# Attention: VectorE's conversions and low parts stand one at a time behind the masks of three steps of a pair, not three in a row in its first step

## The chip, the cores and the metric

The kernel runs on one core of a Trainium2 chip. The metric is the device time of one execution in microseconds (us); for the kernel before it is 1143.96, the median of three runs (1143.52 to 1143.96). Engines are named as in the profile: PE is TensorE (its weight loads are PEld), DVE VectorE, ACT ScalarE, POOL GpSimd, SP SyncE, which here only issues transfers.

## What is computed

Attention with a threshold (scores more than tau below the row's maximum are dropped), then two feed-forward layers on the result.

```python
# q, k, v: (4, 8, 576, 64)
scores = scale * np.matmul(q, k.transpose(0, 1, 3, 2))
thresh = np.max(scores, axis=-1, keepdims=True) - tau
scores = np.where(scores >= thresh, scores, -1000000000.0)
attn = np.exp(scores - np.max(scores, axis=-1, keepdims=True))
attn = attn / (np.sum(attn, axis=-1, keepdims=True) + 1e-09)
x = np.matmul(attn, v)               # then (2304, 512), heads side by side
# first layer:  x = (sigmoid(x @ w_gate) * (x @ w_val)) @ w_out,  d_ff 1536
# second layer: h = x @ w_in;  g = h, 0 or (h + 1)^2 / 4 by range;  out = g @ w_out,  d_ff 2048
```

The weights come as 64-bit floats and are read as pairs of 32-bit words. The kernel makes 32-bit floats of them itself, and splits operands of the feed-forward layers into a high part and a low part (value minus high part).

## The kernel before

**Pairs and steps.** Two heads make a pair; there are 16 pairs, 0 to 15. The 576 rows of a head are four blocks of 128 and a rest of 64, so a pair has five steps, u = 0 to 4; in the last one the rests of both heads share a block. The loop of `attention` (L388 on) runs over steps t = 5p + u, 80 in all and some to drain. It is a pipeline over three steps. In step t stand, on their engines:

- TensorE: the scores of step t (L252; L248 in step 4), the *turns* of step t - 2 (transposes of the probabilities p, L295, and of their last 64 columns lt, L296), and part of the product with v of an earlier block (`attend`, L319).
- VectorE: the *maxima* of step t (L261, one instruction a head: it scales the scores out of PSUM into s and takes the row maximum), then the *masks* of step t - 1 (L281, one a head: threshold, times the exponent, row sum). In step 1 a reciprocal (L333) stands between them.
- ScalarE: the copies of the transposed blocks (L301, L305; L310, L311), the exponents of step t (L273), the copies out of the product with v (L329).
- GpSimd: a shift of the maxima by tau (L264), the copy of the mask's last columns into lt (L288), and the normalisation (L350) two pairs later.

Scores use two banks (wa, wb) in every step, so those of step t + 1 overwrite a bank once VectorE's maxima of step t have read it. Step 4 has one maxima instruction, and step 0 one mask instruction, for the predecessor's step 4; its turns stand in step 1.

**Work beside it.** Weights of the first layer are converted during the attention, six pieces of 128 x 512, by the generator `background` (L352): ScalarE takes out the high words (`extract`, L145, in step 2 of every second pair), and `convert` makes six VectorE instructions of a piece: L155, L157, L159, L161, L165, L169, each building on the one before. Two raw tiles alternate (`load_w`, L129). A call of `next(bg)` advances the generator to its next `yield`. In the loop such a call stands in step 0 of pairs 1 to 12, between the maxima and the mask, and advances by three instructions, so a piece takes two pairs: L155, L157, L159 in the odd one, L161, L165, L169 in the even one.

In pairs 13 to 15 the loop hands out a "gap" at the same place, and `ffn` fills it with VectorE's half of splits: low parts of x (L477, 128 x 768) two in pair 13 and two in pair 14, of weights (L192, 128 x 512) three in pair 15. ScalarE's half, the high parts, was issued at the end of the step ahead (step 4 of pairs 12, 13 and 14). The engines run their instructions in the order of the program; nothing reorders them.

Of the kernel before, what the change touches and what calls it, by code (L numbers as in the profile page):

```python
# [29 lines left out]
def kernel(  # L30
# [57 lines left out]
    high0 = const.tile([P, KD * P], F32, name="high0")  # L88
# [7 lines left out]
    w32 = {(0, 0, 0): ring[0], (0, 0, 1): ring[1]}  # L96
# [12 lines left out]
    def run(*gens):  # L109
        for g in gens:  # L110
            for _ in g:
                pass
# [28 lines left out]
    def extract(ph, gs, c):  # L141

        n = KD * P
        for i, g in enumerate(gs):
            nc.scalar.activation(  # L145
                c[:, i * n : (i + 1) * n], raws[ph, g][:, :, 1].bitcast(F32), AF.Copy, scale=2.0**-112
            )

    def convert(ph, gs, c, a):


        n = KD * P
        c, a = c[:, : len(gs) * n], a[:, : len(gs) * n]
        cu, au = c.bitcast(U32), a.bitcast(U32)
        nc.vector.tensor_scalar(c, c, -DBL_TOP, DBL_TOP, op0=ALU.max, op1=ALU.min)  # L155
        yield
        nc.vector.tensor_scalar(au, cu, 3, None, op0=ALU.logical_shift_left)  # L157
        yield
        nc.vector.scalar_tensor_tensor(au, cu, 0x80000000, au, op0=ALU.bitwise_and, op1=ALU.bitwise_or)  # L159
        yield  # L160
        nc.vector.tensor_scalar(cu, au, 0xFF800000, None, op0=ALU.bitwise_and)  # L161
        yield
        for i, g in enumerate(gs):
            ci = c[:, i * n : (i + 1) * n]
            nc.vector.scalar_tensor_tensor(  # L165
                ci, raws.pop((ph, g))[:, :, 0], 2.0**-52, ci, op0=ALU.mult, op1=ALU.mult
            )
            yield
        nc.vector.tensor_tensor(a, a, c, op=ALU.add)  # L169
        yield  # L170
# [29 lines left out]
    def attention():  # L200
# [14 lines left out]
        U = nf + 1  # L215
        N = NP * U
# [135 lines left out]
        def background():  # L352

            for g in range(2):
                load_w(0, g)
            yield
            for g in range(6):
                extract(0, (g,), high0)
                yield
                n = KD * P  # L360
                ops = convert(0, (g,), high0, w32[0, 0, g // 3][:, g % 3 * n : (g % 3 + 1) * n])
                run(itertools.islice(ops, 3))
                yield
                run(ops)
                if g + 2 < 6:
                    load_w(0, g + 2)
                yield

        def warm(n):

# [13 lines left out]
        bg = background()  # L384
# [7 lines left out]
        for t in range(N + 9):  # L392
            p, u = divmod(t, U)
            on = t < N
            mk = divmod(t - 1, U) if 1 <= t <= N else None
            at = divmod(t - 2, U) if 2 <= t <= N + 1 else None

            pd, ud = divmod(t - U, U)
            pd2, ud2 = divmod(t - 2 * U, U)
            if ud2 in (2, 3) and 0 <= pd2 < NP:  # L400
                normalise(pd2, ud2 - 2)
            if on:
                scores(p, u)
            if t == N + 1:
                yield t - N, True
            if at:
                turns(*at)
            if ud == 2 and 0 <= pd < NP:
                nc.tensor.transpose(left[: 2 * nf + 1, P : 2 * P], sums[pd % 2], ident)
            for part in parts.get(t, ()):  # L410
                attend(*part)
            if on:
                maxima(p, u)
            if at:
                copies(*at)
            if on:
                exponents(p, u)
            if ud == 1 and 0 <= pd < NP:
                denom(pd)
            if on and u == 0 and p > 0:  # L420
                if p < 13:
                    next(bg, None)
                else:
                    yield t - N, "gap"
            if ud == 2 and 0 <= pd < NP:
                sum_rows(pd)
            for part in parts.get(t, ()):
                if part[2][-1] == nf:
                    drain(*part[:2])
            if mk:  # L430
                masks(*mk)
                if mk[1] == nf:
                    nc.gpsimd.tensor_scalar(sums[mk[0] % 2], sums[mk[0] % 2], 1e-9, None, op0=ALU.add)
            if on:
                if u == 1 and p + 1 < NP:
                    corner(p + 1)
                if u == 2 and p + 2 < NP:
                    load(p + 2)
                if u == 4 and p + 2 < NP:
                    load_v(p + 2)  # L440
                if t == 1 or u == 2 and p % 2 == 0 and p < 12:
                    next(bg, None)
            if ud == 3 and 0 <= pd < NP:
                spread(pd)
            if t == N - 1:
                wides[:] = [wb, wa, wt]
            if t == N:
                run(bg)
                nc.scalar.activation(dummy, half, AF.Sigmoid)
                st1.close()  # L450
            if t == N + 2:
                st2.close()
                ps_o.close()
            yield t - N, False

    def ffn(att):


        with ExitStack() as st:
# [340 lines left out]
                            up(0, 0, 0, n, i, pv[i], [kk])  # L800
                        yield

            early, taken, xops = {}, [], {}
            more = first_up()
            ahead = [split_xs(0, 0, 0, T, [c]) for c in range(KD)] + split_list(0, 0, 0, False)
            second = iter(())
            for step, free in att:
                if free == "gap":
                    for g in begun:
                        run(g)  # L810
                    continue
                if free:
                    late = sb("late", 1)
                    wins.append(late.tile([P, 4 * KD * P], F32R, name="win_1"))
                    wouts.extend(late.tile([P, 2, DM], F32R, name=f"wout_{i}") for i in (1, 2))
                    hp_ = sb("hp_", 2)
                    pools["words"] = cv("words", 1).tile([P, 12 * KD * P], F32, name="words")
                    pools["n"] = 0
                    for _, _, gs in todo[:2]:
                        for g in gs:  # L820
                            load_w(0, g)
                    continue
                if step in (-16, -11, -6):
                    begun, ahead = (ahead[:2], ahead[2:]) if step < -6 else (ahead, [])
                    for g in begun:
                        next(g)
                if step == 1:
                    second = split_parts(0, 0, 1, False)
                if step >= 0:
                    run(itertools.islice(second, 2))  # L830
                    run(itertools.islice(more, {0: 4, 1: 2, 2: 2}.get(step, 0)))
# [7 lines left out]
            n = 2 * KD * P  # L839
            slots = [wmore[:, i * n : (i + 1) * n] for i in range(4)] + [x[:, :n] for x in ring]  # L840
            n = 3 * KD * P
# [7 lines left out]
            for s in range(NS):  # L849
                nxt = order[s + 1] if s + 1 < NS else None  # L850
                ops = 8 if order[s][1] == 0 else 6
# [25 lines left out]
                _, t, f = order[s - 1]  # L877
# [74 lines left out]
```

## Time and profile before

| | |
|---|---|
| median of three runs | 1143.96 us |
| profiled execution | 1143.82 us |
| its span, first to last instruction | 1142.0 us |
| busy: PE, DVE, ACT, POOL | 1109.9, 849.0, 620.9, 138.1 us |
| attention, pairs 1 to 15 | 20.4 to 283.7 us of the span |

The profile has pages of totals and views of the trace. A row of a timeline gives the start in us from the span's start, the duration, the engine, the line of the kernel, the operation with its tiles and sizes, and the count of instructions merged in the row; in brackets stands the engine's idle time just before it and what ended that. Matmuls are pipelined and their ends are modelled, so starts are to be trusted more than durations on PE.

### The profile page before, as it was taken

The page shows a single profiled execution, that of the slowest core. Times are in us where ns is not written, and L with a number is a line of the kernel's source. Part 1 is how long each engine was busy: PE and PEld are TensorE (multiplying, and loading weights), DVE is VectorE, ACT ScalarE, POOL GpSimd, SP SyncE. Part 2 cuts the span into 40 slices and gives each one's busy share as a digit, 9 for nine tenths or more (in the row PEclk, how much of TensorE's full clock was granted, in tenths as well). Part 3 has the DMA queues.
Part 4 walks back from the last instruction along what each step waited for, and adds up shares of the span by engine and source line. Part 5 has one row for each costly group of instructions (what it writes and reads, how often), then busy time and mean ns, then how long its engine had stood idle before and what let it go on. Part 6 is the DMA issues. An engine that isn't in the chain of part 4 may idle for free.

```text
span 1142.0 us, 17341 instructions
## 1 busy us (share of the span) xinstructions
PE 1109.9 (97%) x6372; PEld 944.5 (83%) x6372; DVE 849.0 (74%) x1484; ACT 620.9 (54%) x1048; POOL 138.1 (12%) x315
## 2 busy tenths in 40 slices
PE   8999999999799999999999999989999999999998
PEld 5555656556699999999999999988888888988887
DVE  6888888888499999767777762576677767676663
ACT  5777777787444344333344322366566655656553
POOL 3444544555100000000000000000000000000000
PEclk9999999999999999999999999999999999999999
DMA  4323233220665566455446524032312432143301
GB/s 131 88 76 89 78 81 78 62 71 21 212 205 177 176 199 231 168 183 178 154 161 212 176 78 162 19 111 86 133 67 104 156 121 97 72 161 114 111 20 55
DMA packets 65141, 139.09 MB, mean 122 GB/s; under 512 B 9616, under 2 KB 35872, under 8 KB 65056
## 3 DMA queue, kind: packets, MB, share of 16 engines
q1 hardware_dynamic: 64912, 137.98, 36.1%
q8 instruction: 50, 0.82, 0.3%
q14 instruction: 35, 0.29, 0.1%
q10 hardware_dynamic: 144, 0.00, 0.0%
HBM read 111.15 MB, written 26.81 MB: 121 GB/s over the span
## 4 chain that ended last, share of the span: by engine, by line
PE 85%; DVE 8%; ACT 3%; issue 2%; DMA 1%; SPq 0%; POOL 0%; DVEq 0%; POOLq 0%; ACTq 0%
PE y L743 15%; PE pu L610 14%; PE y L761 13%; PE pgv L486 8%; PE pgv L485 8%; PE pgv L487 8%; PE av L319 6%; PE w L295 5%; PE w L252 5%; DVE s L261 2%; PE w L248 2%; DVE p L281 1%; DVE high L165 1%; ACT sqs L619 1%; ACT sqs L620 1%
## 5 line engine op out<-in xcount | busy, mean ns | idle before, releaser
L485 PE MATMUL pgv<-xflat,win 128*128 128x384 f32 x560 | 188.5, 337 | 5.9 <-ACT act L541 3.8
L486 PE MATMUL pgv<-xflat,win 128*128 128x384 f32 x560 | 188.4, 336 | 0.1
L743 PE MATMUL y<-wout,hh 128*128 128x512 f32 x576 | 185.4, 397 | 3.0 <-ACT hh L628 3.0
L487 PE MATMUL pgv<-xflat,win 128*128 128x384 f32 x560 | 188.3, 336 | 0.0
L761 PE MATMUL y<-hh,wout 128*128 128x512 f32 (+1 forms) x576 | 146.7, 337 | 0.0
L261 DVE TENSOR_SCALAR_CACHE_REDUCE s<-w,nscale 128x576 f32<-128x576 f32 x144 | 112.7, 816 | 33.6 <-PE w L252 23.8
L743 PEld LDWEIGHTS y<-wout,hh 128*128 128x128 f32 x576 | 108.9, 189 | 28.0 <-ACT hh L628 3.3
L545 DVE TENSOR_TENSOR act<-pgv,act 128x384 f32<-128x384 f32 x70 | 38.9, 556 | 104.2 <-PE pgv L487 103.9
L743 PE MATMUL y<-wout,hl 128*128 128x512 f32 x288 | 114.3, 397 | 0.5 <-DVE hl L629 0.5
L485 PEld LDWEIGHTS pgv<-xflat,win 128*128 128x128 f32 x560 | 105.9, 189 | 7.9 <-ACT act L541 4.1
L281 DVE SCALAR_TENSOR_TENSOR p<-s,mx,ex 128x576 f32<-128x576 f32 x144 | 112.1, 812 | 0.5 <-POOL lt L288 0.5
L541 ACT ACTIVATE act<-pgv 128x384 f32<-128x384 f32 x70 | 34.2, 489 | 137.1 <-PE pgv L487 136.8
L273 ACT ACTIVATE ex<-s,mx 128x576 f32<-128x576 f32 x144 | 104.8, 775 | 7.2 <-DVE s L261 6.8
L486 PEld LDWEIGHTS pgv<-xflat,win 128*128 128x128 f32 x560 | 106.0, 189 | 2.0 <-DVE xflat L477 0.4
L761 PEld LDWEIGHTS y<-hh,wout 128*128 128x128 f32 x576 | 98.1, 188 | 11.3
L610 PE MATMUL pu<-xflat,win 128*128 128x384 f32 x576 | 105.1, 337 | 1.0 <-DVE sqs L689 0.7
L487 PEld LDWEIGHTS pgv<-xflat,win 128*128 128x128 f32 x560 | 106.0, 189 | 0.0
L546 ACT ACTIVATE hh<-act 128x384 fp32r<-128x384 f32 x72 | 38.0, 527 | 121.7 <-DVE act L545 121.3
L610 PEld LDWEIGHTS pu<-xflat,win 128*128 128x128 f32 x576 | 100.6, 188 | 2.4 <-DVE sqs L689 1.4
L295 PEld LDWEIGHTS w<-ident,p 128*128 128x128 f32 x576 | 62.8, 141 | 41.6 <-ACT ex L273 36.6
L761 PE MATMUL y<-hl,wout 128*128 128x512 f32 (+1 forms) x288 | 97.1, 337 | 0.0
L301 ACT ACTIVATE r<-w 128x1024 f32<-128x1024 f32 x64 | 65.7, 1026 | 49.7 <-PE w L295 49.6
(140 smaller groups left out, 1928.6 us busy)
## 6 DMA issues: line engine op xcount, KB each, us to landing
wmore<-saved SPq DMA_DIRECT2D x32, 512.0 KB
words<-in_moe_w_out_dram SPq DMA_DIRECT2D x26, 512.0 KB
tsum<-tsaved SPq DMA_DIRECT2D x24, 512.0 KB
wmore<-saved SPq DMA_DIRECT2D x15, 768.0 KB
words<-in_moe_w_in_dram SPq DMA_DIRECT2D x16, 512.0 KB
saved<-w SPq DMA_DIRECT2D x16, 512.0 KB
w<-saved SPq DMA_DIRECT2D x16, 512.0 KB
w<-saved SPq DMA_DIRECT2D x9, 768.0 KB
```

Source lines behind the costliest of these rows:

```text
L261: nc.vector.tensor_scalar(t[:, e], w[:, :, :HS], nscale, None, op0=ALU.mult, op1=ALU.min, accum_out=mx[:, 0, e : e + 1])
L273: nc.scalar.activation(ex[:, e], t[:, e], AF.Exp, scale=-1.0, bias=mx[:, 0, e : e + 1])
L281: nc.vector.scalar_tensor_tensor(pr[:, e], t[:, e].rearrange("p a b -> p (a b)"), mx[:, 1, e : e + 1], ex[:, e].rearrange("p a b -> p (a b ...
L295: nc.tensor.transpose(wt[:, e, cs], pr[:, e, cs], ident)
L301: nc.scalar.activation(rt[r].rearrange("p e c n -> p (e c) n")[:, :, o : o + P], wt.rearrange("p e (c n) -> p (e c) n", n=P), AF.Copy,)
L319: nc.tensor.matmul(av[e * D : e * D + D, :n], vs[p % 3][:, e, c], rt[r][:, e, c] if c < nf else rl[r], start=c == 0, stop=c == nf,)
L485: nc.tensor.matmul(ps, ih[:, i, kk], xh[:, kk, c], start=(kk == 0), stop=False)
L486: nc.tensor.matmul(ps, ih[:, i, kk], xl[:, kk, c], start=False, stop=False)
L487: nc.tensor.matmul(ps, il[:, i, kk], xh[:, kk, c], start=False, stop=(kk == KD - 1))
L610: nc.tensor.matmul(ps[bank], l[:, k], r[:, k], start=bool(new) and k == m == 0, stop=k == HK - 1 and m == 2, skip_group_check=True,)
L743: nc.tensor.matmul(y[b], l[:, ts_], r, start=first and m == 0, stop=last and m == 2)
L761: nc.tensor.matmul(at(y, a, b), l[:, ds_], r[:, c], start=new and m == 0, stop=last and m == 2, skip_group_check=True,)
```

## The change

The calls leave step 0's place between maxima and mask. They stand behind the masks now, in steps 0, 3 and 4 of a pair, from t = 3 on, and `background` yields after each single instruction of `convert`. The six instructions of a piece begin in step 3 of the pair in which it was extracted; a piece still ends in step 0 of pairs 2, 4, ... 12. The next raw tile's load is issued with the next extraction (step 2) instead of behind the sixth instruction (step 0). For the low parts the "gap" comes from t = 63 on in the same three steps, and one part is taken each time.

```diff
--- before.py
+++ after.py
@@ -358,13 +358,9 @@
                 extract(0, (g,), high0)
                 yield
                 n = KD * P
-                ops = convert(0, (g,), high0, w32[0, 0, g // 3][:, g % 3 * n : (g % 3 + 1) * n])
-                run(itertools.islice(ops, 3))
-                yield
-                run(ops)
+                yield from convert(0, (g,), high0, w32[0, 0, g // 3][:, g % 3 * n : (g % 3 + 1) * n])
                 if g + 2 < 6:
                     load_w(0, g + 2)
-                yield
 
         def warm(n):
 
@@ -417,11 +413,6 @@
                 exponents(p, u)
             if ud == 1 and 0 <= pd < NP:
                 denom(pd)
-            if on and u == 0 and p > 0:
-                if p < 13:
-                    next(bg, None)
-                else:
-                    yield t - N, "gap"
             if ud == 2 and 0 <= pd < NP:
                 sum_rows(pd)
             for part in parts.get(t, ()):
@@ -431,6 +422,11 @@
                 masks(*mk)
                 if mk[1] == nf:
                     nc.gpsimd.tensor_scalar(sums[mk[0] % 2], sums[mk[0] % 2], 1e-9, None, op0=ALU.add)
+            if on and u in (0, 3, 4) and t > 2:
+                if t <= 12 * U:
+                    next(bg, None)
+                else:
+                    yield t - N, "gap"
             if on:
                 if u == 1 and p + 1 < NP:
                     corner(p + 1)
@@ -800,14 +796,14 @@
                             up(0, 0, 0, n, i, pv[i], [kk])
                         yield
 
-            early, taken, xops = {}, [], {}
+            early, taken, xops, begun = {}, [], {}, []
             more = first_up()
             ahead = [split_xs(0, 0, 0, T, [c]) for c in range(KD)] + split_list(0, 0, 0, False)
             second = iter(())
             for step, free in att:
                 if free == "gap":
-                    for g in begun:
-                        run(g)
+                    run(*begun[:1])
+                    del begun[:1]
                     continue
                 if free:
                     late = sb("late", 1)
```

VectorE's instructions in steps 0 and 1 around pair 5, before (s, mx: maxima; p, sum: masks; high, w: conversions):

```order
L261 TENSOR_SCALAR s,mx_77<-w_126,nscale 128x576
L261 TENSOR_SCALAR s,mx_77<-w_127,nscale 128x576
L155 TENSOR_SCALAR high_84<-high_84 128x512
L157 TENSOR_SCALAR w_0_82<-high_84 128x512
L159 SCALAR_TENSOR_TENSOR w_0_82<-high_84,w_0_82 128x512
L281 SCALAR_TENSOR_TENSOR p,sum_80<-s,mx_76,ex 128x576
L261 TENSOR_SCALAR s,mx_76<-w_126,nscale 128x576
```

The same place now, first step 0, then steps 3 and 4 (between them stand the maxima and masks of steps 1 to 3):

```order
L261 TENSOR_SCALAR s,mx_77<-w_126,nscale 128x576
L261 TENSOR_SCALAR s,mx_77<-w_127,nscale 128x576
L281 SCALAR_TENSOR_TENSOR p,sum_80<-s,mx_76,ex 128x576
L159 SCALAR_TENSOR_TENSOR w_0_82<-high_84,w_0_82 128x512
L261 TENSOR_SCALAR s,mx_76<-w_126,nscale 128x576
```

```order
L281 SCALAR_TENSOR_TENSOR p,sum_81<-s,mx_77,ex 128x576 x2
L161 TENSOR_SCALAR high_84<-w_0_82 128x512
L261 TENSOR_SCALAR s,mx_77<-w_126,nscale 128x576
L281 SCALAR_TENSOR_TENSOR p,sum_81<-s,mx_76,ex 128x576 x2
L165 SCALAR_TENSOR_TENSOR high_84<-raw_86,high_84 128x512
L261 TENSOR_SCALAR s,mx_76<-w_126,nscale 128x576
```

L155 and L157 moved ahead, to steps 3 and 4 of pair 4; L159 stands behind the mask; L161 and L165, which stood in pair 6, follow in steps 3 and 4 of pair 5.

VectorE in step 0 of pair 13, before (xflat: low parts of x):

```order
L261 TENSOR_SCALAR s,mx_77<-w_126,nscale 128x576
L261 TENSOR_SCALAR s,mx_77<-w_127,nscale 128x576
L477 TENSOR_TENSOR xflat<-xall,xflat 128x768 x2
L281 SCALAR_TENSOR_TENSOR p,sum_80<-s,mx_76,ex 128x576
L261 TENSOR_SCALAR s,mx_76<-w_126,nscale 128x576
L261 TENSOR_SCALAR s,mx_76<-w_127,nscale 128x576
```

VectorE from step 3 of pair 13 to step 1 of pair 14, now (the low parts have line 473 in the changed file):

```order
L261 TENSOR_SCALAR s,mx_76<-w_126,nscale 128x576
L261 TENSOR_SCALAR s,mx_76<-w_127,nscale 128x576
L281 SCALAR_TENSOR_TENSOR p,sum_81<-s,mx_77,ex 128x576 x2
L473 TENSOR_TENSOR xflat<-xall,xflat 128x768
L261 TENSOR_SCALAR s,mx_77<-w_126,nscale 128x576
L281 SCALAR_TENSOR_TENSOR p,sum_81<-s,mx_76,ex 128x576 x2
L261 TENSOR_SCALAR s,mx_76<-w_126,nscale 128x576
L261 TENSOR_SCALAR s,mx_76<-w_127,nscale 128x576
L281 SCALAR_TENSOR_TENSOR p,sum_81<-s,mx_77,ex 128x576
L473 TENSOR_TENSOR xflat<-xall,xflat 128x768
L261 TENSOR_SCALAR s,mx_77<-w_126,nscale 128x576
```

The second low part of pair 13 moved from step 0 to step 3; the first one of pair 14 stands behind the mask of step 0.

SyncE's transfers between the loads of v and the spreading of the reciprocals (rb), in pairs 1 and 2, before:

```order
L236 DMA v_164<-in_v_dram 64x64
L129 DMA raw_86<-in_moe_w_out_dram 128x1024
L340 DMA dr<-row_79 9x128
L226 DMA qk<-in_q_dram 128x576
L227 DMA qk<-in_k_dram 128x576
L346 DMA rb<-dr 128x1x512
```

And now:

```order
L236 DMA v_164<-in_v_dram 64x64
L340 DMA dr<-row_79 9x128
L226 DMA qk<-in_q_dram 128x576
L227 DMA qk<-in_k_dram 128x576
L129 DMA raw_86<-in_moe_w_out_dram 128x1024
L346 DMA rb<-dr 128x1x512
```

The raw tile's load moved behind the reciprocals' rows (dr) and the loads of q and k; the same holds for four such loads in all.

## Rows read from the trace of the kernel before

**Rows 1.** Stretches: length, busy us (instructions) by engine, granted clock, DMA share, GB/s.

```profile
...
20.40:283.70 263.30, 250.37 (x1770) 155.78 (x1770) 232.63 (x603) 197.34 (x372) 125.48 (x282) 1.00 0.26 70
...
313.50:318.00 4.50, 4.47 (x16) 4.30 (x17) 3.84 (x5) 1.90 (x4) 0.00 (x0) 0.62 1.02 325
...
```

**Rows 2.** Groups of PE in 20.4 to 283.7 us: busy, mean ns | idle before.

```profile
...
L295 PE MATMUL w<-ident,p 128*128 128x128 f32 x540 | 74.2, 278 | 12.9 <-DVE p L281 10.1 <-ACT ex L273 2.8
...
```

**Rows 3.** Timeline of PE, pairs 1, 5, 6 and 13.

```profile
...
25.99 0.63 PE L295 MATMUL w<-ident,p 128*128 128x128 f32 x4 [0.97 <-DVE p L281]
...
90.76 1.24 PE L252 MATMUL w<-qk 64*128 64x288 f32 x8
91.94 1.09 PE L295 MATMUL w<-ident,p 128*128 128x128 f32 x8
92.87 0.27 PE L296 MATMUL left<-ident,lt 128*128 128x128 f32 x1
...
94.08 1.24 PE L252 MATMUL w<-qk 64*128 64x288 f32 x8
96.01 0.63 PE L295 MATMUL w<-ident,p 128*128 128x128 f32 x4 [0.69 <-DVE p L281]
96.47 0.27 PE L296 MATMUL left<-ident,lt 128*128 128x128 f32 x1
...
106.37 1.04 PE L295 MATMUL w<-ident,p 128*128 128x128 f32 x8
...
108.14 1.24 PE L252 MATMUL w<-qk 64*128 64x288 f32 x8
...
113.65 0.63 PE L295 MATMUL w<-ident,p 128*128 128x128 f32 x4 [0.95 <-DVE p L281]
...
236.26 0.63 PE L295 MATMUL w<-ident,p 128*128 128x128 f32 x4 [0.90 <-ACT ex L273]
...
```

**Rows 4.** Timeline of DVE, pairs 1, 5, 6 and 13.

```profile
...
22.02 0.82 DVE L261 TENSOR_SCALAR_CACHE_REDUCE s<-w,nscale 128x576 f32<-128x576 f32 x1
...
93.52 0.42 DVE L155 TENSOR_SCALAR high<-high 128x512 f32<-128x512 f32 x1
...
94.43 0.69 DVE L159 SCALAR_TENSOR_TENSOR w<-high,w 128x512 uint32<-128x512 uint32 x1
95.04 0.81 DVE L281 SCALAR_TENSOR_TENSOR p<-s,mx,ex 128x576 f32<-128x576 f32 x1
...
106.57 0.82 DVE L261 TENSOR_SCALAR_CACHE_REDUCE s<-w,nscale 128x576 f32<-128x576 f32 x1 [0.49 <-PE w L248]
...
107.32 0.82 DVE L281 SCALAR_TENSOR_TENSOR p<-s,mx,ex 128x576 f32<-128x576 f32 x1
...
108.06 0.82 DVE L281 SCALAR_TENSOR_TENSOR p<-s,mx,ex 128x576 f32<-128x576 f32 x1
...
109.41 0.82 DVE L261 TENSOR_SCALAR_CACHE_REDUCE s<-w,nscale 128x576 f32<-128x576 f32 x1 [0.53 <-PE w L252]
...
110.89 0.42 DVE L161 TENSOR_SCALAR high<-w 128x512 uint32<-128x512 uint32 x1
111.35 0.69 DVE L165 SCALAR_TENSOR_TENSOR high<-raw,high 128x512 f32<-128x512 uint32 x1
...
112.68 0.81 DVE L281 SCALAR_TENSOR_TENSOR p<-s,mx,ex 128x576 f32<-128x576 f32 x1
...
233.56 1.82 DVE L477 TENSOR_TENSOR xflat<-xall,xflat 128x768 fp32r<-128x768 f32 x2
...
```

**Rows 5.** Timeline of POOL, pair 5.

```profile
...
106.22 0.29 POOL L288 COPY lt<-p 128x128 f32<-128x128 f32 x1 [0.73 <-DVE p L281]
107.57 0.71 POOL L264 TENSOR_SCALAR mx<-mx,tau_b 128x1 f32<-128x1 f32 x1 [1.06 <-DVE s L261]
...
```

**Rows 6.** Timeline of ACT, pair 5.

```profile
...
94.14 1.44 ACT L273 ACTIVATE ex<-s,mx 128x576 f32<-128x576 f32 x2
...
105.14 1.44 ACT L273 ACTIVATE ex<-s,mx 128x576 f32<-128x576 f32 x2
...
```

## The prediction

> **What bounds the kernel now.** I read the stages first: busy time and granted clock of each engine in the attention's fifteen pairs after the first, 20.4 to 283.7 us [rows 1]. TensorE is busy for 250.37 of 263.30 us there, at full clock, so 12.93 us is all that TensorE can gain in the stage by waiting less; VectorE is at 232.63, close, but not full. The second view, TensorE's groups of the same stretch, says where the 12.93 us lie: 12.9 stand before the turns (L295) and 10.1 of these were ended by a VectorE mask (L281) [rows 2]. The third view is TensorE's timeline of pair 5 [rows 3]. Call the starts of its five steps S0 to S4: the scores open a step. From S0 = 90.76 to S1 = 94.08 TensorE has no gap. In step 1 the scores start at 94.08, the turns could follow at 95.25 (in step 0 they follow 1.18 us after the scores' start: 91.94 - 90.76), but start at 96.01. From there to the next pair at 108.14 no gap is marked. So each pair waits once, in step 1, for the mask of the pair's predecessor.
>
> VectorE's timeline says why [rows 4]: between the two maxima of step 0 and that mask stand three conversions, 93.52 to 95.04, and the mask can start only then. In even pairs the three take 110.89 to 112.68, 1.79 us for 1.52, and the wait is 0.95 for 0.69 [rows 3, 4]. In pairs 13 to 15 low parts stand there (two in 1.82 us at 233.56, wait 0.90) [rows 3, 4].
>
> **The change part by part.** *Removed: the wait in step 1.* The mask now follows the maxima at once. In pair 5 it starts at 93.52 instead of 95.04 and is over, by its own 0.74 us from start to the next start (its neighbour L281 at 107.32 hands over at 108.06), at 94.26. The turns followed the mask's start by 0.97 (112.68 to 113.65), so they could start at 94.49, and TensorE reaches them at 95.25. The whole wait goes, with 0.76 us to spare. Sum over the pairs of the recorded waits: pair 1 0.97, five odd pairs 0.69, six even 0.95, pairs 13 to 15 0.90 to 0.97: 12.9. A recorded wait counts from the modelled end of the scores, 1.24 us after their start, while TensorE goes on after 1.18 when nothing is in the way; that is some 0.06 to 0.07 more a pair, 1.0 in all. **Gain 13.9 us.** TensorE is next in every step of the pair; I looked at each of the moved instructions for one that takes its place.
>
> *Added in step 0, behind the mask:* one conversion of at most 0.69 us (L159), from 94.26 to 94.95. The next maxima wait for their scores until some 95.35 (scores 94.08, and 1.27 to 1.28 from scores to maxima, as 108.14 to 109.41). Hidden, 0.4 us spare.
>
> *Added in step 3, behind two masks:* L155 or L161, 0.42 us, taking 0.46 with its hand-over (110.89 to the next conversion at 111.35). VectorE idles 0.49 us there, before the maxima at 106.57. Hidden. A low part in its place (0.91 each) makes those maxima 0.3 to 0.4 late, in three places.
>
> *Added in step 4:* L157 (0.45 with its hand-over, 0.91 less 0.46) or L165 (0.69, 0.72 with its hand-over) into an idle time of 0.53 before 109.41. L165 starts at 108.80, lasts until some 109.52 and makes the maxima 0.1 late in the odd pairs. A late maximum costs TensorE nothing until it holds up the scores of the step after: the maxima of 109.41 end by 110.89, and the scores that overwrite their banks stand at 111.46 or later (3.32 after 108.14). 0.1 fits, and so does 0.3 in step 3, where one maximum ends at 107.32 and the next scores stand at 108.14. I take zero; the bound, if the late maxima of the low parts show in full, is 1 us.
>
> *Moved in the first pair.* Two conversions now stand in steps 3 and 4 of pair 0. There VectorE is the bound: the maxima at 22.02 follow a mask without a marked idle time [rows 4]. So the two, 0.91 us with their hand-overs (93.52 to 94.43), push the maxima of pair 1's step 0 to 22.9, their end to 24.4 and the scores of step 1 to some 24.4 to 24.6; the turns then start at about 25.6 instead of 25.99 [rows 3]. Of the 1.04 us that I counted for pair 1 only 0.4 is left: **loss 0.65 us**, between 0 and 0.9.
>
> *Moved on SyncE:* four of the weight loads (512 KB) stand two steps later, behind the q and k loads and ahead of the reciprocals' spreading. The tile is read two pairs later, the spread rows four steps later, and the moved load waits for nothing by then (its buffer's last reader ran three steps before). Nothing; what it could cost is a late spread, in at most four pairs.
>
> *GpSimd.* It copies the last columns of a mask (L288, lt) for TensorE and shifts the maxima (L264). A small operation with nothing beside it takes 0.29 us (106.22); one that began at 107.57 inside the mask of 107.32 took 0.71, to 0.22 us after that mask was over [rows 4, 5]. So an operation with two inputs in SBUF on VectorE holds GpSimd up. The Trainium skill says so too ("SBUF — State Buffer", "Who interferes with whom"): a VectorE instruction with two SBUF inputs, or a tensor_scalar in the two-port mode, and a GpSimd instruction exclude each other for the whole instruction. By that rule this change puts a blocker right where the copy of lt starts, which speaks against it. In this kernel's rows it comes to: in step 0 the conversion ends at 94.95, L264 and L288 come after it, 0.28 + 0.29, 95.52; TensorE takes lt at 95.25 + 0.46 (four turns, 96.01 to 96.47) = 95.71. In step 4 the conversion ends at 109.52 and lt at 110.1; TensorE wants it 2.11 us after 108.14 (90.76 to 92.87), at 110.25. Both fit by 0.15 to 0.2 us. I take zero; if it misses by 0.1 in each of 15 pairs, 1.5 us.
>
> **Sum:** 13.9 - 0.65 = 13.2 us. The profiled execution took 1143.82 (span 1142.0 and 1.8 around it), the median of the runs is 1143.96; from the median, **1130.8 us**.
>
> *After the attention* nothing changes its place; everything starts 13 us earlier. One thing there is not rigid: the granted clock, 1.00 in the attention, is 0.62 on average from 313.5 to 318.0 us [rows 1], a mixture of the levels 2.4 and 1.2 GHz, behind idle times of TensorE. That costs 4.5 x 0.38 = 1.7 us, and can come out otherwise: 2 us either way.
>
> **The rivals.** *A: ScalarE takes the mask's place.* The exponents of step 0 run from 94.14 to 95.58 [rows 6], and 2.8 of the 12.9 us are put down to exponents, in pairs 13 to 15 [rows 2, 3]. If the turns needed them, they would start at about 95.68, 0.43 late, in 15 pairs 6.5 us: **1137.3**. Against it: in step 4 the turns start at 106.37 while exponents run from 105.14 to 106.58 [rows 3, 6]. With it goes the milder form of the bounds above (VectorE or GpSimd late by 0.2 to 0.4 a pair, 1134 to 1137).
>
> *B: GpSimd's copy gets no turn until the maxima behind the conversion are over.* That ends slower. In step 0 lt would be there at 95.35 + 1.48 + 0.29 = 97.1 instead of 95.7, 1.4 late; in step 4 at 109.52 + 1.48 + 0.29 = 111.3, 1.0 late; in step 3 some 0.35. Together 2.8 a pair against 0.93 saved: 15 x 1.9 = 28 us, **1172**. It decides against the change from 0.3 us a step on. Against it: the row of 107.57 ends 0.22 us after the mask, though VectorE went straight on to another one.
>
> *C: the gain is given back behind the attention*, because the feed-forward part waits for transfers that don't move: **1143.9**. For it: the chain of waits runs through a transfer of saved weights there. Against it: this transfer is queued behind the last pair's spread, so it moves along. That the change does not do what it says is ruled out by the instruction order, where the three conversions do stand apart.
>
> **How the numbers follow.** Forecast 0.78, A and its milder forms 0.13, C 0.05, B 0.04. The forecast's own range is 1128.5 to 1133 (clock 2 us, bounds of 0 to 2.5 us on the other side). To hold 8 in 10 with a part of A: 1128.3 to 1136. About 0.2% (2.3 us) is what a measurement of this kernel can tell from no change. Faster by more: 0.91 (forecast and A); within: 0.05 (C); slower: 0.04 (B).
>
> **What would show it.** Right: TensorE's groups of the attention show under 1 us of waiting before L295 from pair 2 on; a pair's pitch is 16.6 us, odd or even, instead of 17.4 and 17.6; the attention's last score is some 13 us earlier; VectorE's idle time before the maxima of steps 3 and 4 is nearly gone. Wrong: marked waits before L296 with GpSimd's copy as releaser (B), before L295 with exponents (A), scores waiting for maxima (VectorE the bound), or a right pitch with an unchanged end (C).

## The result, and the profile after

The changed kernel takes 1131.39 us (median of four runs, 1129.67 to 1131.77) against 1143.96 us (four runs beside it, 1143.52 to 1148.13): ratio 0.988, 95% interval 0.985 to 0.990. The forecast was 1130.8, the range 1128.3 to 1136.0. The profiled execution took 1131.51 us, its span is 1129.7. Here are the 12.3 us between the two spans, stage by stage ("last turns" are the last eight of the attention, L295; "first wait" is the end of TensorE's first long wait in the feed-forward part, 3.75 us in the changed kernel):

| stretch | before | after | difference |
|---|---|---|---|
| start to the scores of step 0, pair 1 | 20.46 | 19.96 | -0.50 |
| from there to the last turns (pairs 1 to 15) | 263.56 | 250.08 | -13.48 |
| last turns to the end of the first wait | 23.71 | 23.99 | +0.28 |
| from there to the end | 834.27 | 835.67 | +1.40 |

The gain is the second row. The 0.50 us of the first row are not the change's: the kernel's first maxima, ahead of anything that the change touches, already came 0.62 earlier in this execution (7.03 us for 7.65).

The stage first, as [rows 1] have it for before: busy time of PE, PEld, DVE, ACT and POOL with the instructions, granted clock, DMA share and GB/s over the attention from pair 1 on.

```profile
...
20.40:270.10 249.70, 249.38 (x1771) 155.51 (x1768) 228.30 (x599) 196.85 (x374) 147.50 (x282) 1.00 0.26 73
...
```

TensorE now idles 0.32 us in the whole stage, where it idled 12.93. It is the bound, and almost nothing is left of the waits. One other column moved much: GpSimd is busy for 147.50 us instead of 125.48, with the same 282 instructions; they take longer.

TensorE's groups from 20.0 to 270.5 us, busy and mean, and behind the bar the idle time ahead of them, say it by line; the first answers to [rows 2]:

```profile
...
L295 PE MATMUL w<-ident,p 128*128 128x128 f32 x544 | 75.3, 279 | 0.3 <-ACT r L301 0.3
L252 PE MATMUL w<-qk 64*128 64x288 f32 x480 | 74.4, 429 | 0.3 <-DVE s L261 0.3
...
```

The 12.9 us ahead of the turns have become 0.3, and these stand in the drain, the steps behind the last scores (270.04). The 0.3 ahead of L252 is a wait that ended before the stage, at 19.96. The timeline of PE, pair 1 and pairs 4 to 6, stands for [rows 3] (start, duration, instruction; an idle time would stand in brackets):

```profile
...
24.45 0.66 PE L295 MATMUL w<-ident,p 128*128 128x128 f32 x4
...
86.54 1.24 PE L252 MATMUL w<-qk 64*128 64x288 f32 x8
...
89.86 1.24 PE L252 MATMUL w<-qk 64*128 64x288 f32 x8
91.03 0.66 PE L295 MATMUL w<-ident,p 128*128 128x128 f32 x4
91.53 0.27 PE L296 MATMUL left<-ident,lt 128*128 128x128 f32 x1
...
103.19 1.24 PE L252 MATMUL w<-qk 64*128 64x288 f32 x8
...
119.83 1.24 PE L252 MATMUL w<-qk 64*128 64x288 f32 x8
...
```

The turns of step 1 follow the scores by 1.17 us (91.03 - 89.86) without a gap. The pitch, from the first scores of a pair to those of the next, is 16.65 and 16.64 us (86.54, 103.19, 119.83), odd or even, where it was 17.4 and 17.6. One interval is longer than it was: the four turns take 0.50 us until L296 (91.03 to 91.53), where 0.46 had been enough behind a wait (96.01 to 96.47 in [rows 3]).

VectorE's timeline, pair 1 and the pairs around 5, stands for [rows 4]:

```profile
...
18.00 0.82 DVE L281 SCALAR_TENSOR_TENSOR p<-s,mx,ex 128x576 f32<-128x576 f32 x1
...
18.75 0.42 DVE L155 TENSOR_SCALAR high<-high 128x512 f32<-128x512 f32 x1
19.09 0.81 DVE L261 TENSOR_SCALAR_CACHE_REDUCE s<-w,nscale 128x576 f32<-128x576 f32 x1
...
84.98 0.82 DVE L261 TENSOR_SCALAR_CACHE_REDUCE s<-w,nscale 128x576 f32<-128x576 f32 x1 [0.15 <-PE w L248]
...
87.81 0.82 DVE L261 TENSOR_SCALAR_CACHE_REDUCE s<-w,nscale 128x576 f32<-128x576 f32 x1 [0.19 <-PE w L252]
...
90.04 0.69 DVE L159 SCALAR_TENSOR_TENSOR w<-high,w 128x512 uint32<-128x512 uint32 x1
91.13 0.82 DVE L261 TENSOR_SCALAR_CACHE_REDUCE s<-w,nscale 128x576 f32<-128x576 f32 x1 [0.41 <-PE w L252]
...
104.46 0.82 DVE L261 TENSOR_SCALAR_CACHE_REDUCE s<-w,nscale 128x576 f32<-128x576 f32 x1
...
```

Each conversion of a steady pair went into idle time ahead of maxima. What is left of that time is 0.15 us ahead of step 4's maxima (84.98; 0.49 before), 0.19 or nothing ahead of the next step 0's (0.53 before; now 87.81, and 104.46 behind L165), and 0.41 ahead of step 1's (91.13). In steady pairs VectorE now has less than half a microsecond to give in any of these places.

GpSimd's timeline stands for [rows 5], ScalarE's for [rows 6]:

```profile
...
89.55 1.25 POOL L264 TENSOR_SCALAR mx<-mx,tau_b 128x1 f32<-128x1 f32 x1 [0.45 <-DVE s L261]
90.73 0.29 POOL L288 COPY lt<-p 128x128 f32<-128x128 f32 x1
...
104.06 0.62 POOL L288 COPY lt<-p 128x128 f32<-128x128 f32 x1 [0.73 <-DVE p L281]
...
```

```profile
...
89.92 1.44 ACT L273 ACTIVATE ex<-s,mx 128x576 f32<-128x576 f32 x2
...
```

L264 of 0.28 us of its own took 1.25, through the mask and L159 (90.04 + 0.69 = 90.73; it ended at 90.80). The copy of lt came after it and ended at 91.02; L296 wanted it at 91.53. Behind L165 (which ends at 104.53) lt ended at 104.68, and TensorE wanted it 2.10 us after 103.19, at 105.29. So GpSimd is held up behind both conversions and still has 0.5 to 0.6 us to spare. And the exponents of step 0 end at 91.36, after the turns of step 1 began (91.03): the turns don't need them. It is the same in pair 15, behind a low part: the turns start at 257.49, the exponents run from 257.00 to 258.46.

Behind the attention, TensorE's first long wait and what follows it, as the second of [rows 1] had it:

```profile
...
290.00:294.03 4.03, 0.28 (x2) 0.00 (x0) 4.03 (x4) 2.57 (x5) 2.19 (x2) 0.77 0.49 191
294.03:298.00 3.97, 3.97 (x12) 3.70 (x12) 3.90 (x6) 0.00 (x0) 0.74 (x1) 0.50 0.17 40
...
299.80:304.00 4.20, 4.18 (x13) 4.18 (x14) 3.54 (x5) 1.90 (x4) 0.00 (x0) 0.50 1.06 313
304.00:306.30 2.30, 2.30 (x11) 2.01 (x10) 2.30 (x3) 1.22 (x3) 0.00 (x0) 0.60 0.35 144
...
```

After 3.75 us without work the granted clock is 0.50, the level of 1.2 GHz, and it stays there until about 306. The kernel before had the same wait, and after it 0.50 for 2.87 us (below) and then, after more waiting, 0.62 over 4.5 us [rows 1].

```profile
...
307.73:310.60 2.87, 2.87 (x9) 2.87 (x10) 2.83 (x5) 0.00 (x0) 0.73 (x1) 0.50 0.06 26
...
```

The work behind the first wait is the same in both kernels. TensorE's next long wait, 2.99 us in both, ends 461.65 us behind the first one before (at 769.38) and 462.83 now (at 756.87), so 1.18 of the 1.40 us in the table's last row arise up to there. Around that second wait the granted clock falls to 0.50 again, for 3.4 us before (771.5 to 774.9) and 6.8 us now (756.4 to 763.2); from its end on the kernel takes the other 0.22 us more.

### The profile page after: what moved, and what is told of

The parts are those of the page before. It is cut to its first block, busy times and chain, and to the rows that moved or that the text cites. A ratio compares the mean times of both kernels' runs of the same rounds, so it can differ in the third digit from the quotient of the medians.

```text
span 1129.7 us, 17350 instructions
## 1 busy us (share of the span) xinstructions
PE 1111.8 (98%) x6372; PEld 946.4 (84%) x6372; DVE 844.5 (75%) x1484; ACT 621.0 (55%) x1048; POOL 160.5 (14%) x315
## 4 chain that ended last, share of the span: by engine, by line
PE 91%; DVE 5%; ACT 2%; issue 1%; POOL 0%; DVEq 0%; POOLq 0%; ACTq 0%
PE y L739 15%; PE pu L606 14%; PE y L757 13%; PE pgv L482 8%; PE pgv L481 8%; PE pgv L483 8%; PE av L319 8%; PE w L252 7%; PE w L295 6%; PE w L248 2%; PE left L296 1%; ACT sqs L615 1%; ACT sqs L616 1%; ACT hh L624 1%; PE av L368 0%
## 5 line engine op out<-in xcount | busy, mean ns | idle before, releaser
L264 POOL TENSOR_SCALAR mx<-mx,tau_b 128x1 f32<-128x1 f32 x144 | 95.1, 664 | 71.3 <-DVE s L261 71.3
```

What stands on the lines that cost most here:

```text
L264: nc.gpsimd.tensor_scalar(mx[:, 1, e : e + 1], mx[:, 0, e : e + 1], tau_b, None, op0=ALU.add)
```

## The experiments

All ratios are against the kernel before on the same chip (1143.48 and 1143.68 us, seven runs each). "Attention" is the table's second stretch, to be compared with 263.56 before and 250.08 after.

| kernel | median us (range) | ratio, 95% interval | attention | from the first wait on |
|---|---|---|---|---|
| e1_row_behind | 1135.2 (1133.62 to 1136.82) | 0.9924, 0.9909 to 0.9938 | 254.75 | 835.42 |
| e2_single_ahead | 1131.79 (1131.3 to 1132.22) | 0.9894, 0.9877 to 0.991 | 251.89 | 833.44 |
| e3_lows_in_row | 1132.19 (1131.67 to 1134.04) | 0.99, 0.9885 to 0.9915 | 252.97 | 834.66 |
| e4_two_inputs | 1131.36 (1131.25 to 1132.7) | 0.989, 0.9874 to 0.9907 | 251.91 | 834.62 |
| e5_one_input | 1131.14 (1128.18 to 1131.44) | 0.9883, 0.9868 to 0.9897 | 250.22 | 835.53 |
| e6_keep_clock | 1128.36 (1127.81 to 1130.39) | 0.9867, 0.9852 to 0.9882 | 250.09 | 832.02 |
| e7_after_again | 1130.37 (1127.91 to 1131.24) | 0.9878, 0.9864 to 0.9893 | 250.08 | 832.33 |
| e8_keep_again | 1128.19 (1127.8 to 1129.04) | 0.9864, 0.9849 to 0.9878 | 250.09 | 832.94 |

The last column moves by 3.3 us between two executions of one kernel (835.67 in the changed kernel, 832.33 in e7), while the attention's length repeats to 0.01 where nothing in it was changed (250.08 in both, 250.09 in e6 and e8). So I judge e1 to e5 by the attention's length in the trace. A microsecond or two in the total time is not evidence on them.

### Only the order: three in a row again, but behind the mask

```diff
-            if on and u in (0, 3, 4) and t > 2:
-                if t <= 12 * U:
-                    next(bg, None)
+            if on and u == 0 and p > 0:
+                if p < 13:
+                    run(itertools.islice(bg, 3))
                 else:
                     yield t - N, "gap"
...
-                    run(*begun[:1])
-                    del begun[:1]
+                    run(*begun)
+                    del begun[:]
```

> The three conversions of a pair (and the two or three low parts of pairs 13 to 15) stand in a row again, in step 0 alone, but behind its mask; everything else as in the changed kernel. My theory: the mask is then as early as in the changed kernel, but the row keeps VectorE until 5.0 us (odd pairs) or 5.3 us (even) after S0 and holds GpSimd's L264 and the copy of lt (L288) up until then, so TensorE waits before L296 of step 1 instead of before L295, some 0.55 us in odd pairs, 0.85 in the others: 6 x 0.55 + 9 x 0.85 = 11 us over the changed kernel, 1142 us, pitch 17.2 and 17.5. Rival theory: only the place behind the mask counts, GpSimd slips in between the conversions; then only the late maxima show, 0.05 to 0.3 a pair, about 1134 us, pitch 16.7 to 16.9.

Measured: 4.67 us more attention than the changed kernel. Moving the row behind the mask alone brings 8.8 of the 13.5 us, and the 1135.2 us are nearer to the rival theory (1134) than to mine (1142). GpSimd, VectorE and TensorE in pair 5 and TensorE later, timeline:

```profile
...
90.88 0.98 POOL L264 TENSOR_SCALAR mx<-mx,tau_b 128x1 f32<-128x1 f32 x1 [0.45 <-DVE s L261]
91.80 0.29 POOL L288 COPY lt<-p 128x128 f32<-128x128 f32 x1
...
```

```profile
...
91.82 0.54 DVE L157 TENSOR_SCALAR w<-high 128x512 uint32<-128x512 uint32 x1
...
93.01 0.81 DVE L261 TENSOR_SCALAR_CACHE_REDUCE s<-w,nscale 128x576 f32<-128x576 f32 x1
...
```

```profile
...
92.86 0.27 PE L296 MATMUL left<-ident,lt 128*128 128x128 f32 x1
...
94.51 1.35 PE L252 MATMUL w<-qk 64*128 64x288 f32 x8
...
228.46 0.33 PE L296 MATMUL left<-ident,lt 128*128 128x128 f32 x1 [0.37 <-POOL lt L288]
...
```

I had expected lt to be held until the whole row was over. In pairs 1 to 12 it was not: GpSimd's two operations ended at 91.86 and 92.09, while VectorE was already at L157, and L157 took 0.54 instead of 0.42. The lt copy was in time (92.86). What costs is the other end: the maxima stand behind three conversions, start at 93.01, and the scores of step 2, which overwrite the banks they read, stretch from 1.24 to 1.35 us, in even pairs to 1.61 (their three conversions are longer). The pitch is 16.74 in the odd pairs from 3 on, 17.02 in the even pairs and 17.03 in pair 1. In pairs 13 and 14, behind low parts, it is 17.24 and 17.23, and there L296 does wait for lt, 0.37 and 0.38. Pair 15 is 0.36 longer up to the last turns. Five times 0.10, seven times 0.38, twice 0.59 and 0.36 are 4.7. So the place behind the mask alone brings two thirds; the next run has the other half alone.

### One at a time, but ahead of the masks

```diff
             if ud == 1 and 0 <= pd < NP:
                 denom(pd)
+            if on and u in (0, 3, 4) and t > 2:
+                if t <= 12 * U:
+                    next(bg, None)
+                else:
+                    yield t - N, "gap"
             if ud == 2 and 0 <= pd < NP:
                 sum_rows(pd)
...
-            if on and u in (0, 3, 4) and t > 2:
-                if t <= 12 * U:
-                    next(bg, None)
-                else:
-                    yield t - N, "gap"
```

> One conversion (or low part) at a time in steps 0, 3 and 4 as in the changed kernel, but ahead of the step's masks, where the row of three stood before. My theory: spreading alone frees TensorE, since one instruction of 0.45 to 0.72 us ahead of a mask fits into the 0.76 us that the mask has to spare in step 0 and into more in steps 3 and 4: 1131 to 1133 us, pitch about 16.65. Rival theory: the mask has to come first; then TensorE waits in step 0's successor for most of the 0.7 us and in the other two steps for part of theirs, 0.4 us a pair or more: 1137 us or more.

Measured: 1.81 us more attention; spreading alone brings 11.7 of the 13.5 us. In pairs 2 to 12 the pitch is 16.64 to 16.67: ahead of the mask one conversion does no harm, as the 0.76 us to spare that the prediction worked out for the mask would have it. It loses at the two ends, TensorE's timeline:

```profile
...
25.26 0.63 PE L295 MATMUL w<-ident,p 128*128 128x128 f32 x4 [0.18 <-DVE p L281]
...
272.20 1.30 PE L295 MATMUL w<-ident,p 128*128 128x128 f32 x8 [0.93 <-DVE p L281]
273.73 0.33 PE L296 MATMUL left<-ident,lt 128*128 128x128 f32 x1 [0.22 <-POOL lt L288]
...
```

Pair 1 waits 0.18, the drain 0.93 and 0.22, where the changed kernel has 0.32 in the drain, and from step 4 of pair 13 to step 4 of pair 14 it takes 16.99 (234.47 to 251.46). From first scores to first scores pair 1 takes 17.08 for 16.65, pairs 13 and 14 16.99 and 16.98, and pair 15 is 0.60 longer up to the last turns: that is 1.7 of the 1.81. There VectorE is full (no idle time is marked ahead of the maxima of step 4 in pair 14, at 253.25), and what stands ahead of a mask is paid for. The median, 1131.79, doesn't show the loss, since this execution got some of it back behind the attention (833.44). So in steady pairs the gain comes from spreading; which side of the mask matters where VectorE is full.

### Conversions spread, low parts in a row as before

```diff
+            if on and u == 0 and p > 12:
+                yield t - N, "gap"
             if ud == 2 and 0 <= pd < NP:
                 sum_rows(pd)
...
-            if on and u in (0, 3, 4) and t > 2:
-                if t <= 12 * U:
-                    next(bg, None)
-                else:
-                    yield t - N, "gap"
+            if on and u in (0, 3, 4) and 2 < t <= 12 * U:
+                next(bg, None)
...
-                    run(*begun[:1])
-                    del begun[:1]
+                    run(*begun)
+                    del begun[:]
```

> The conversions stand as in the changed kernel, the low parts of pairs 13 to 15 in a row in step 0 ahead of the mask as before. My theory: the three waits of these pairs come back, 0.90 to 0.97 us by the rows plus 0.04 to 0.07 for the modelled ends, 2.9 us in all: 1134.3 us. If the low parts' waits were put down to ScalarE's exponents rightly (rival A), they did not go away with the change and come back as nothing: 1131.4 us, with the waits in both kernels.

Measured: 2.89 us more attention, all of it in three waits: TensorE's, then VectorE's mask and ScalarE's exponents ahead of the first of them.

```profile
...
226.07 0.63 PE L295 MATMUL w<-ident,p 128*128 128x128 f32 x4 [0.90 <-ACT ex L273]
...
261.31 0.63 PE L295 MATMUL w<-ident,p 128*128 128x128 f32 x4 [0.97 <-ACT ex L273]
...
```

```profile
...
225.10 0.81 DVE L281 SCALAR_TENSOR_TENSOR p<-s,mx,ex 128x576 f32<-128x576 f32 x1
...
```

```profile
...
224.50 1.46 ACT L273 ACTIVATE ex<-s,mx 128x576 f32<-128x576 f32 x2
...
```

0.90, 0.90 and 0.97 are the waits of the kernel before, and the profile puts them down to exponents as it did there [rows 2, 3]. Mask and exponents end within 0.05 us of each other (225.91 and 225.96), so the name went to the wrong one: the turns started 0.97 after the mask's start, as at 113.65 in [rows 3], the waits came and went with the low parts ahead of the mask, and in the changed kernel these turns start before such exponents end (257.49 and 258.46). The three pairs carry 2.9 of the 13.5 us, pairs 1 to 12 the rest.

### GpSimd's lock measured: one more instruction behind the conversion

Behind L159 or L169, in step 0 of pairs 1 to 12, one more VectorE instruction of 128x576 that nobody needs: in e4 with two inputs in SBUF, in e5 with one; both also write an accumulator. Tile `spare` is filled once, ahead of the loop.

```diff
...
                 if t <= 12 * U:
                     next(bg, None)
+                    if u == 0:
+                        nc.vector.scalar_tensor_tensor(
+                            spare[:, 1200:1776], spare[:, :576], 1.0, spare[:, 600:1176], op0=ALU.mult, op1=ALU.max,
+                            accum_out=dummy,
+                        )
...
```

```diff
...
                 if t <= 12 * U:
                     next(bg, None)
+                    if u == 0:
+                        nc.vector.tensor_scalar(
+                            spare[:, 1200:1776], spare[:, :576], nscale, None, op0=ALU.mult, op1=ALU.min, accum_out=dummy,
+                        )
...
```

> The changed kernel with one more VectorE instruction behind the conversion in step 0 of pairs 1 to 12: a scalar_tensor_tensor of 128 x 576 on a tile of its own, with two inputs in SBUF, 0.74 us from start to start. My theory: GpSimd can't read SBUF while such instructions follow each other without a gap, so L264 and the copy of lt (L288) come 0.23 and 0.29 us after the added instruction (ended 4.85 to 4.95 us after S0), 0.35 to 0.45 us later than TensorE wants lt (4.99); a wait before L296 with L288 as its releaser in twelve pairs, 4 to 5 us: about 1136 us. Rival theory: GpSimd gets its turn between the conversion and the added instruction, as it did between the conversions of the row behind the mask; then no wait before L296 and 1131 to 1132 us.

> As e4_two_inputs, but the added instruction is a tensor_scalar of 128 x 576 with one input in SBUF that also accumulates, of the same 0.74 us. Both theories: it doesn't hold GpSimd up; L264 and L288 run beside it, no wait before L296; the maxima of step 1 are 0.3 us late, which TensorE doesn't notice: 1131 to 1132 us, pitch 16.65. The difference to e4_two_inputs is the price of the second input alone.

Measured: e5 250.22, 0.14 from the changed kernel; e4 1.69 us more than e5, 0.14 a pair, where 4 to 5 had been expected. GpSimd, VectorE and TensorE in pair 5 (L265, L289 and L297 here are L264, L288 and L296 of the changed kernel, L296 the turns), first e4:

```profile
...
90.76 1.24 POOL L265 TENSOR_SCALAR mx<-mx,tau_b 128x1 f32<-128x1 f32 x1 [0.45 <-DVE s L262]
91.95 0.81 POOL L289 COPY lt<-p 128x128 f32<-128x128 f32 x1
...
```

```profile
...
91.85 0.75 DVE L431 SCALAR_TENSOR_TENSOR spare<-spare 128x576 f32<-128x576 f32 x1
...
```

```profile
...
92.25 0.66 PE L296 MATMUL w<-ident,p 128*128 128x128 f32 x4
92.81 0.33 PE L297 MATMUL left<-ident,lt 128*128 128x128 f32 x1
...
```

and e5:

```profile
...
89.56 1.25 POOL L265 TENSOR_SCALAR mx<-mx,tau_b 128x1 f32<-128x1 f32 x1 [0.45 <-DVE s L262]
90.75 0.28 POOL L289 COPY lt<-p 128x128 f32<-128x128 f32 x1
...
```

```profile
...
90.65 0.80 DVE L431 TENSOR_SCALAR_CACHE_REDUCE spare<-spare,nscale 128x576 f32<-128x576 f32 x1
...
```

Beside an instruction with one SBUF input the copy of lt runs in 0.28 us; beside one with two it takes 0.81 and ends at 92.76, 0.16 after that instruction (92.60). The Trainium skill has this rule ("SBUF — State Buffer", "Who interferes with whom"): a VectorE instruction with two SBUF inputs contends with a GpSimd instruction that reads SBUF, and one with at most one SBUF input, outside the two-port modes, does not. The pair of runs agrees with it, 0.81 us against 0.28. The price came out small because only one of GpSimd's two operations was left behind the added instruction; L265 had slipped in between L159 and L431 and ended at 92.00. Then lt missed TensorE by under a tenth: L297 stands 0.56 after the turns instead of 0.49 and takes 0.33 instead of 0.27. The two are the 0.13 by which the pitch grew, 16.77 for 16.64.

### The clock behind the attention

Twenty-six matmuls of the identity, whose result is never read, stand in TensorE's two waits behind the attention.

```diff
+            def keep(n):
+                for _ in range(n):
+                    nc.tensor.matmul(wides[0][:, 0, :P], ident, ident, start=True, stop=True)
...
+                        if (t, f, n) == (0, 1, 1):
+                            keep(14)
                         up(0, t, f, n, 0, pg)
                         nc.scalar.activation(act, pg, AF.Sigmoid)
+                        if (t, f, n) == (0, 1, 1):
+                            keep(12)
                         up(0, t, f, n, 1, pv)
```

> The changed kernel with 26 idle matmuls (128 x 128, into a bank that nobody reads, 0.12 us per pass at full clock) in the two idle times of TensorE behind the attention: 14 ahead of the sixth group of the first layer, 12 ahead of the seventh. My theory: in the changed kernel TensorE is granted 1.2 GHz from 294.0 to 306 us because it stood idle for 3.75 and 1.58 us; with something to do it stays at 2.4 GHz, the 12 matmuls behind the first idle time are hidden by VectorE's chain anyway, and the stretch from 299.8 to 306.1 is 3 us shorter: 1128.4 us. Rival theory: the low clock there does not come from the idle times, or idle matmuls don't count: 1131.4 us and the same granted clock, or longer if the fillers hold up the work behind them.

To separate this from differences between executions it was repeated beside the changed kernel (e7), on one chip, as e8.

> The changed kernel once more, on the same chip as the next one: 1131.4 us, with the stretch behind the attention at 1.2 GHz for 6 to 12 us, and its end 1 us to either side according to that.

> The changed kernel with the 26 idle matmuls in TensorE's idle times behind the attention (e6_keep_clock) once more, beside the changed kernel on the same chip: 3 us less than that, 1128.4 us, if the low clock comes from the idle times; 1131.4 us if the first result was luck of the clock.

Stretches behind the attention, columns as in [rows 1], first e6, then e7:

```profile
...
290.00:294.00 4.00, 3.41 (x30) 3.21 (x28) 4.00 (x4) 2.59 (x5) 2.21 (x2) 1.00 0.37 143
294.00:298.00 4.00, 3.92 (x28) 3.92 (x29) 3.93 (x6) 0.03 (x1) 0.77 (x1) 1.00 0.15 38
298.00:302.00 4.00, 3.30 (x23) 3.11 (x22) 3.34 (x4) 2.37 (x4) 0.00 (x0) 1.00 1.03 305
...
```

```profile
...
290.00:294.00 4.00, 0.25 (x2) 0.23 (x2) 4.00 (x5) 2.57 (x5) 2.36 (x2) 1.00 0.40 154
294.00:298.00 4.00, 3.47 (x12) 2.96 (x11) 3.93 (x5) 0.00 (x0) 0.52 (x1) 0.57 0.21 53
298.00:302.00 4.00, 2.42 (x13) 2.40 (x14) 3.34 (x5) 2.37 (x4) 0.00 (x0) 1.00 1.07 312
...
```

With the fillers the clock is 1.00 throughout these stretches, and the waits themselves stay where they were (TensorE's useful work resumes at 294.08, in the changed kernel at 294.03): they cost no time. Without them it falls to 1.2 GHz for 3.4 us in one execution (e7, 294.4 to 297.8, in the view 0.57 on average over 4 us), and stays there until about 306 in another (after). The medians are 1128.36 and 1128.19 with the fillers and 1131.39 and 1130.37 without, 1128.19 against 1130.37 on one chip; the ranges of e7 and e8 overlap (1127.91 is among e7's runs) and so do their intervals. So about 2 us at the median, and less spread; that the fillers are never slower isn't shown by so few runs.

The traces say where the difference lies. From the end of the first wait to the end of the next long one (2.99 us, at 753.9 to 756.9 in these four) it takes 460.08 and 460.14 us with the fillers (e6, e8), 462.83 (after) and 460.15 (e7) without: the fillers give what e7 had by luck. At that next wait, where there are none, the clock falls in every run, e6 and e8 too, for 3.4 or 6.8 us; that moves the last column as well, and no run put fillers there.

## Why the prediction was right, point by point

**What bounds the kernel**: right. TensorE's waits in the attention were all there was to gain, and 12.6 of the 12.93 us went.

**The gain of 13.9**: 13.48. The pitch was to be TensorE's own 16.62, and is 16.64 to 16.65. With no wait ahead of them four turns take 0.50 until L296 instead of 0.46, so the interval I took from behind a wait was some 0.03 to 0.04 too short: 15 x 0.03 = 0.4. No run changed that interval alone.

**The first pair, a loss of 0.65**: mis-sized; it is about 0.12. The scores of pair 1 came 0.50 earlier than before while the first maxima of the kernel, ahead of anything the change touches, came 0.62 earlier (7.03 for 7.65 us). I had added each conversion at 0.45 behind the mask. But maxima straight behind a mask start late anyway; VectorE's timeline of the kernel before, pair 0:

```profile
...
18.63 0.81 DVE L281 SCALAR_TENSOR_TENSOR p<-s,mx,ex 128x576 f32<-128x576 f32 x1
...
19.58 0.82 DVE L261 TENSOR_SCALAR_CACHE_REDUCE s<-w,nscale 128x576 f32<-128x576 f32 x1
...
```

That is 0.95 from start to start, where two masks stand 0.74 apart, and no idle time is marked. With the conversion in between it is 1.09 (18.00, 18.75, 19.09): it adds 0.14, not 0.45. The pair's turns, at 24.45, wait for nothing.

**Steps 0, 3 and 4 hidden, GpSimd zero**: right, and the bounds of 1 and 1.5 us weren't called on. Where I allowed lt 0.15 to 0.2 us to spare it has 0.5 to 0.6: in step 0 L264 ends 0.07 behind the conversion (90.80) and lt 0.22 later, where I had let both run at full length, 0.28 and 0.29, from the conversion's end on; in step 4 lt ends 0.15 behind it. One place in the drain does pay: the last low part (L192) holds lt to 271.17, and L296 stands 1.18 us after the last turns instead of 0.93. That is the table's 0.28.

**Moved on SyncE, nothing**: right as far as the trace goes. No instruction on TensorE, VectorE, ScalarE or GpSimd is marked as waiting for a transfer in pairs 1 to 15, before or now. The moved loads were not tested apart from the rest.

**After the attention**: the allowance of 2 us either way was right, and it was used: +1.40 in the profiled execution, while another execution of the same kernel (e7) came out at -1.9. The prediction looked at one place with a low clock; the second long wait, 462 us later, is another.

**The sum**, in the profiled executions: -13.90 + 0.42 (pitch) + 0.12 (first pair) - 0.62 (ahead of it) + 0.28 (drain) + 1.40 (clock) = -12.30. Forecast was -13.2; by the medians it is -12.6. The change's own terms come to -13.08. That the total lies within 0.6 us of the forecast is in part luck: the errors in the pitch and the drain and the one in the first pair have opposite signs, and so have the early start and the clock, which belong to the execution and not to the change.

**The rivals.** A (exponents take the mask's place) fell: the turns start before those exponents end. B (lt gets no turn until the maxima are over) fell: in step 4 lt ends 0.15 us behind the conversion, with maxima running (from 104.46), and in step 0 some 0.3 behind it, before the maxima start. Its mechanism is there, one instruction deep: e4 makes lt miss, for 0.14 a pair. C (given back behind the attention) fell: the first wait ends at 294.03 instead of 307.73, so the transfers moved along.

## What to carry to other kernels

Small work that may run anywhere belongs where its engine idles ahead of the same wait in each step, one instruction at a time; in a row ahead of the one instruction that the bounding engine waits for, all is paid that goes beyond what this instruction had to spare (here 1.52 us of conversions against 0.76). In the trace, count the idle time of the helping engine by place before moving work there: three places of about 0.5 us took three instructions, and the same three in one place did not fit (e1). When two releasers end as close together as here (0.05 us in e3), the name the profile gives is weak evidence; move one of them and see. And before a difference of a microsecond or two is put down to a change, look at the granted clock in stretches that the change left alone.

## What was not expected of the hardware

- A conversion between a mask and the maxima on VectorE cost 0.14 us instead of its 0.42 in pair 0, since these maxima start 0.95 us behind a mask's start and 0.34 behind the conversion's. Ahead of a mask, behind maxima, the next such conversion cost 0.34 (e2, 20.17 to 20.51). What the 0.2 us are was not tested. The maxima write the buffer (mx) that the mask ahead of them has just read, as the lists of VectorE's order have it, and they start 0.14 behind its end (19.44, 19.58): that they wait for this end fits, but is not shown.
- GpSimd gets in where one VectorE instruction follows another: in e1 L264 and L288 ended at 91.86 and 92.09 while a new conversion had begun at 91.82, and that took 0.54 instead of 0.42 us; in e4 L265 got in and the next operation did not. Which of two it will be was not settled.
- Behind the same wait of 3.75 us the granted clock was 0.50 for about 12 us in one execution and for 3.4 us in another of the same kernel; fillers in the wait kept it at 1.00. At the next long wait, 2.99 us, it fell to 0.50 in all ten profiled executions, for 3.4 us in four and 6.8 us in six.
